# Scores of all heads in native fp32, two heads on the two row halves of the PE array

## The chip, the core and the metric

The program runs on one NeuronCore of a Trainium2 chip. The metric is the device time of one execution in microseconds (us). Five engines run their own instruction streams and wait for each other through semaphores: TensorE (PE; the weight loads of its matmuls are listed apart as PEld), VectorE (DVE), ScalarE (ACT), GpSimd (POOL) and SyncE (SP, which issues the DMAs here).

## What is computed

Causal attention for 4 batches of 12 heads, 448 positions and head size 64, then a gated feed-forward layer on the 1792 tokens. The inputs are float32 and the weights of the second part float64.

```python
scores = scale * np.matmul(q, k.transpose(0, 1, 3, 2))
mask = np.triu(np.ones((seq, seq), dtype=bool), k=1)
scores = np.where(mask, -1000000000.0, scores)
scores = scores - np.max(scores, axis=-1, keepdims=True)
attn = np.exp(scores)
attn = attn / (np.sum(attn, axis=-1, keepdims=True) + 1e-09)
out = np.matmul(attn, v)                  # (4, 12, 448, 64) -> x (1792, 768)
g = x @ w_gate                            # (768, 1536)
val = x @ w_val
y = (g * (1.0 / (1.0 + np.exp(-g))) * val) @ w_out
```

## The kernel before

**Chunks and units.** The work is cut into four chunks, one for each batch. A chunk has 12 attention units (one head each, taken two by two as pairs) and then a feed-forward part of 36 weight tiles (`moe`, L638). The feed-forward part of chunk c is meant to run together with the attention of chunk c+1, so that TensorE always has matmuls.

**A unit.** The 448 queries are cut into four blocks of 64, 128, 128 and 128 rows; block i needs the keys up to its own end (64, 192, 320, 448). For each block a score matmul fills an S bank of PSUM (L423), DVE adds the mask and takes the row maximum (L440), ACT takes the exponential with the row sums (L449), DVE adds and inverts the sums (L460, L461), and one of three engines scales the rows (L470, L474, L478). Then, for each block of keys j, TensorE transposes the probabilities into a T bank (L501), ACT copies them to SBUF (L268), in most units DVE writes the rest after rounding (L290), and the product with v is summed in an O bank (L514, or L533 and L535). The result is written into `xs`, the input of the feed-forward part.

**Two ways to keep float32 precision.** A matmul on float32 operands ("native") is slower for each column than one on `fp32r` operands (float32 rounded to fewer bits). So a product can also be split: an operand is written as a rounded part and a rest, and matmuls on the parts are summed. `NS` says pair by pair whether the scores are native ("n") or split ("s"): native in batch 0, split in batches 1 to 3. Both forms of a score matmul have 128 rows here. In the split form q is rounded into `QS` on rows 0 to 63 (L399), its rest goes to rows 64 to 127 (L400), k goes rounded into `KH` (L402) and its rest into `KL` (L403), and two matmuls with QS give the block (L429, L430). In the native form k is zero on rows 64 to 127, and one matmul gives the block (L426); the trace has two records for it. `NP` chooses in the same manner for the product with v. The feed-forward part is split throughout, three matmuls of 448 columns for a product (L634 to L636), which is why every weight tile is first rebuilt from float64 on DVE (L604, L608, L612; `wraw`) and split (`whl`: copy at L268 or L274, rest at L290 or L293) in chunk 0, stored to DRAM, and loaded again for the later chunks.

**The order.** The program for each engine is an order that a list scheduler written out in the kernel (`Planner`, L81) makes before the build. Each operation has one or more engines with an estimated cost (`cost`, L51), a due time, the operations that it needs, and the buffers that it takes; `CAPS` says how many buffers (or PSUM banks: S, T, O, M) a tag has. The scheduler gives each operation to the engine where it would end first, with a bias for each engine. Each engine then works through its list in that order.

**Loads.** q and k are given twice, on both halves of the partitions; a pair's q or k is one DMA of 128 rows x 2 heads x 448 (448 KB), but for the first pair, which is loaded head by head.

Of the kernel before, what the change touches and what calls it, by code (L numbers as in the profile page):

```python
# [15 lines left out]
D = 64  # L16
# [10 lines left out]
NS = ['nn', 's', 'sss', 'sss']  # L27
# [8 lines left out]
TM = 0  # L36
OM = 0
SM = 1
# [27 lines left out]
class Op:  # L66
    __slots__ = ("port", "soft", "alts", "due", "deps", "alloc", "uses", "extra", "idx", "nd", "outs", "start", "end", "eng", "fn")
# [13 lines left out]
class Planner:  # L81
# [9 lines left out]
    def run(self, caps):  # L91
        free = dict.fromkeys(("PE", "DVE", "ACT", "POOL", "SP"), 0.0)
        ring = {}
        lock = {"DVE": 0.0, "POOL": 0.0}

# [20 lines left out]
        def ready(o, e):  # L116
            t = 0.0
            for d in o.deps:
                x = d.end if d in o.soft else d.end + d.extra + (LAT if d.eng != e else (0.0 if e == "PE" else 0.1))
                if x > t:  # L120
                    t = x
            for r in o.alloc:
                q = slots(r.tag)
                h = q[0]
# [16 lines left out]
        def choose(e):  # L141
# [23 lines left out]
        while left:  # L165
# [10 lines left out]
            o.end = s + o.alts[e][0]  # L176
            o.fn = o.alts[e][1]
            free[e] = o.end
            if e == "POOL" or (e == "DVE" and o.port):
                lock[e] = o.end  # L180
# [4 lines left out]
            for r in o.uses:  # L185
                r.left -= 1
                r.end = max(r.end, o.end + o.extra + LAT)
# [14 lines left out]
def kernel(  # L202
# [9 lines left out]
    B, _, H, S = qT.shape  # L212
# [44 lines left out]
    def op(alts, due, deps=(), alloc=(), uses=(), extra=0.0):  # L257
# [3 lines left out]
        o.port = bool(alts.pop("port", False))  # L261
        for r in alloc:
            heads[r.tag] = o
# [33 lines left out]
    class Unit:  # L297
        def __init__(self, c, b, h, qa, qb, col):
# [6 lines left out]
            self.ns, self.np = nat(NS, b, h), nat(NP, b, h)  # L305
# [28 lines left out]
    loads = {}  # L334
    xs_ops, xs_res, xlast = {}, {}, {}

    def attention(u):
# [3 lines left out]
        ns, npv = U.ns, U.np  # L341
# [4 lines left out]
        if h % 2 == 0:  # L346
            def make(nm):
                if nm == "v":
                    t = buf([P, 2, NKC, D], F32, "vraw", "vraw", f"vraw{u}")[:, :, :nj]
                else:  # L350
                    t = buf([P, 2, S], F32, nm + "raw", nm + "raw", f"{nm}raw{u}")
                    t = t[:, :, :N] if nm == "q" else t[:, :, :KB]
                st[u][nm], st[u + 1][nm] = t[:, 0], t[:, 1]
                return t

            def src(nm, hs):
                if nm == "v":
                    return vP[b, :, hs, :nj]
                return qT[b, :, hs, U.qa : U.qb] if nm == "q" else kT[b, :, hs, :KB]

            def both(nm):
                def go():
                    t = make(nm)
                    nc.sync.dma_start(t, src(nm, slice(h, h + 2)))
                r = Res(nm + "raw")
                o = op({"SP": (0.6, go)}, base - 8.0, alloc=[r], extra=3.0)
                loads[u, nm] = loads[u + 1, nm] = (o, r)

            def one(nm, first):
                def go():  # L370
                    if first:
                        make(nm)
                    nc.sync.dma_start(st[u + 1 - first][nm], src(nm, h + 1 - first))
                if first:
                    r = Res(nm + "raw")
                    loads[u, nm] = (op({"SP": (0.6, go)}, base - 8.0, alloc=[r], extra=2.5), r)
                else:
                    o, r = loads[u, nm]
                    loads[u + 1, nm] = (op({"SP": (0.6, go)}, base - 8.0, [o], uses=[r], extra=2.5), r)

            if u == 0:
                for first in (1, 0):
                    for nm in "qk":
                        one(nm, first)
                both("v")
            else:
                for nm in "qkv":
                    both(nm)
# [4 lines left out]
        if not ns:  # L393
            rQ, rKH, rKL = Res("QS"), Res("KH"), Res("KL")

            def new(tag):
                s[tag] = buf([P, S], F32R, tag, tag, f"{tag}{u}")[:, : N if tag == "QS" else KB]
                return s[tag]
# [17 lines left out]
        exps, rps = [], {}  # L416
        for i, (q0, q1_) in U.qi:
            r, o0 = q1_ - q0, q0 - U.qa
            stag = "M" if c == 0 and SM and i == 3 else "S"
            sl = U.pslot(q1_)  # L420
            rS, rp = Res(stag), Res(f"p{sl}")

            def score(i=i, o0=o0, q1_=q1_, r=r, stag=stag):  # L423
                S_ = s[f"S{i}"] = bank(stag, f"S{u}_{i}")
                if ns:
                    nc.tensor.matmul(S_[:r, :q1_], s["q"][:, o0 : o0 + r], s["k"][:, :q1_], start=True, stop=True)  # L426
                else:
# [4 lines left out]
            if ns:  # L432
                so = op({"PE": (cost("PE", "n", q1_), score)}, due(2), [lq, lk], [rS], [rq, rk])
            else:
                so = op({"PE": (2 * cost("PE", "r", q1_), score)}, due(2), [q2, k2], [rS], [rQ, rKH, rKL])
# [48 lines left out]
        otag = "M" if c == 0 and OM and h % 2 else "O"  # L484
        rO = Res(otag)
        last = None
        pvs = []
        for j in range(nj):
            k0, k1_ = U.kb[j]
            bs, sl, stk = U.base(j), U.slot(j), U.stacked(j)  # L490
            kn, n = k1_ - k0, U.qb - bs
            lastj = j == nj - 1
            ttag = "M" if c == 0 and TM and j % 2 else "T"
            rT, rh = Res(ttag), Res(f"ph{sl}")
            qs = [(i, e) for i, e in U.qi if e[0] >= k0]

            def transp(j=j, k0=k0, k1_=k1_, kn=kn, ttag=ttag, qs=qs, bs=bs):
                pt = s[f"T{j}"] = bank(ttag, f"T{u}_{j}")
                for i, (q0, q1_) in qs:
                    r = q1_ - q0  # L500
                    nc.tensor.transpose(pt[:kn, q0 - bs : q1_ - bs], s[f"p{i}"][:r, k0:k1_], ident[:r, :r])  # L501
            tr = op({"PE": (sum(cost("PE", "t", max(kn, e[1] - e[0])) for _, e in qs), transp)}, due(7),
                    [norms[i] for i, _ in qs], [rT], [rps[i] for i, _ in qs])

            def newh(j=j, n=n, kn=kn, sl=sl):
                s[f"ph{j}"] = buf([P, S - WID[sl]], F32 if npv else F32R, f"ph{sl}", "ph", f"ph{u}_{j}")[:, :n]
                return s[f"ph{j}"][:kn]
            hi = op(copies("psum", n, newh, lambda j=j, kn=kn, n=n: s[f"T{j}"][:kn, :n],
                           engines="AD" if npv else "A"), due(8), [tr], [rh], [rT])
            if npv:  # L510
                def pv(j=j, kn=kn, bs=bs, lastj=lastj):
                    if j == 0:
                        s["O"] = bank(otag, f"O{u}")
                    nc.tensor.matmul(s["O"][:D, bs - U.qa : N], s["v"][:kn, j], s[f"ph{j}"][:kn],  # L514
                                     start=(j == 0), stop=lastj)
                pvs.append((cost("PE", "n", n), pv, [hi, lv], [rh, rv]))
                continue
            rl = None if stk else Res(f"pl{sl}")

            def newl(j=j, n=n, kn=kn, sl=sl, stk=stk):  # L520
                if stk:
                    return s[f"ph{j}"][kn : 2 * kn]
                s[f"pl{j}"] = buf([P, S - WID[sl]], F32R, f"pl{sl}", "pl", f"pl{u}_{j}")[:, :n]
                return s[f"pl{j}"][:kn]
            lo = op(binary(n, newl, lambda j=j, kn=kn, n=n: s[f"T{j}"][:kn, :n],
                           lambda j=j, kn=kn: raw(s[f"ph{j}"])[:kn], engines="D"),
                    due(9), [hi], [] if stk else [rl], [rT, rh])

            def pv(j=j, bs=bs, stk=stk, lastj=lastj):
# [249 lines left out]
```

## Time and profile before

| | us |
|---|---|
| median of 3 runs | 769.82 (769.75 to 773.38) |
| profiled execution | 767.99 |
| its span, first to last instruction | 766.2 |
| PE busy | 729.5 |
| DVE busy | 446.0 |
| ACT busy | 387.7 |
| POOL busy | 241.4 |

The profile is one execution. A busy time is the length of the union of an engine's records; records of matmuls overlap, so the time that a matmul costs is read from one start to the next start. In the rows below, "128\*64" behind a matmul is rows x columns of its stationary operand, and the last number of a shape is the columns that it streams. "x8" is a count of merged records; a row of merged records carries the shape of the first alone.

### The profile page before, as it was taken

The numbers are of one execution on the slowest core, as the hardware profiler recorded it, in microseconds if no ns is written. First come the engines' busy times: TensorE is split into PE (matmuls) and PEld (weight loads), VectorE is DVE, ScalarE is ACT, GpSimd is POOL, SyncE is SP. The second block draws the span as 40 slices with busy tenths as digits, with TensorE's granted clock in tenths as the row PEclk, the third lists the DMA queues.
The fourth block names the chain that finished last, engine by engine and source line by source line (L and its number), as shares of the span: only waits on it lengthen the run. The fifth ranks groups of instructions, "written<-read, shape, count | busy, mean of one in ns | idle before, by whom it ended". The sixth has DMA issues, their size and how long they took to land.

```text
span 766.2 us, 10921 instructions
## 1 busy us (share of the span) xinstructions
PE 729.5 (95%) x3798; PEld 632.2 (83%) x3798; DVE 446.0 (58%) x1009; ACT 387.7 (51%) x979; POOL 241.4 (32%) x291
## 2 busy tenths in 40 slices
PE   6999978788889899999999999999999999999998
PEld 3556867677768799998998999898998999999997
DVE  3878989998999875555564426556564322222100
ACT  5888566677767665445464435545455431111100
POOL 3577546455454463123232212322223100000000
PEclk9999999999999999999999999999999999999999
DMA  8645888687889986656556675655545566665672
GB/s 331 208 151 183 271 281 295 222 331 258 308 269 332 337 306 223 224 199 208 199 204 224 227 234 205 225 200 192 187 162 174 189 197 231 220 213 209 208 263 92
DMA packets 40087, 176.09 MB, mean 230 GB/s; under 512 B 4448, under 2 KB 8032, under 8 KB 40032
## 3 DMA queue, kind: packets, MB, share of 16 engines
q1 hardware_dynamic: 40032, 175.39, 66.3%
q8 instruction: 30, 0.49, 0.2%
q14 instruction: 25, 0.20, 0.1%
HBM read 141.56 MB, written 33.82 MB: 229 GB/s over the span
## 4 chain that ended last, share of the span: by engine, by line
PE 78%; DVE 11%; DMA 4%; ACT 3%; issue 2%; POOL 1%; SPq 0%; POOLq 0%; ACTq 0%; DVEq 0%
PE M L634 13%; PE M L636 12%; PE M L635 12%; PE T L501 7%; PE MO L634 7%; PE MO L636 7%; PE MO L635 7%; DVE wraw L608 3%; PE S L426 3%; PE O L533 3%; DVE wraw L612 2%; PE S L429 2%; PE S L430 2%; PE O L535 2%; DMA wide<-in_w_dram 2%
## 5 line engine op out<-in xcount | busy, mean ns | idle before, releaser
L636 PE MATMUL M<-xh,whl 128*128 128x448 f32 x576 | 212.0, 368 | 7.5 <-DVE whl L290 7.5
L634 PE MATMUL M<-xh,whl 128*128 128x448 f32 x576 | 215.8, 375 | 0.0
L635 PE MATMUL M<-xl,whl 128*128 128x448 f32 x576 | 211.1, 366 | 0.5 <-DVE xl L290 0.5
L636 PEld LDWEIGHTS M<-xh,whl 128*128 128x128 f32 x576 | 108.5, 188 | 19.4 <-DVE whl L290 10.4
L449 ACT ACTIVATE p<-p,m 64x64 f32<-64x64 f32 x192 | 95.9, 501 | 40.7 <-DVE m L440 40.5
L635 PEld LDWEIGHTS M<-xl,whl 128*128 128x128 f32 x576 | 108.9, 189 | 8.6 <-DVE xl L290 0.9
L634 PEld LDWEIGHTS M<-xh,whl 128*128 128x128 f32 x576 | 109.0, 189 | 7.6 <-issue 0.2
L268 ACT ACTIVATE ph<-T 64x448 fp32r<-64x448 f32 (+1 forms) x192 | 72.6, 416 | 79.6 <-PE T L501 78.3
L440 DVE CUSTOM_DVE_ANT_0 p<-S,mask 64x64 f32<-64x64 f32 x192 | 76.5, 417 | 61.3 <-PE S L430 42.7
L636 PE MATMUL MO<-hh,whl 128*128 128x448 f32 x288 | 106.0, 368 | 4.3 <-DVE whl L290 4.2
L634 PE MATMUL MO<-hh,whl 128*128 128x448 f32 x288 | 107.5, 373 | 0.0
L635 PE MATMUL MO<-hl,whl 128*128 128x448 f32 x288 | 105.5, 366 | 0.0
L501 PE MATMUL T<-ident,p 128*128 128x128 f32 (+2 forms) x480 | 80.2, 279 | 10.3 <-DVE ph L290 5.4
L501 PEld LDWEIGHTS T<-ident,p 128*128 128x128 f32 (+2 forms) x480 | 53.2, 130 | 44.5 <-issue 12.0
L474 POOL TENSOR_SCALAR p<-p,rec 128x448 f32<-128x448 f32 (+3 forms) x77 | 45.0, 594 | 74.3 <-DVE rec L461 56.9
L290 DVE TENSOR_TENSOR pl<-T,ph 128x384 fp32r<-128x384 f32 (+2 forms) x126 | 50.1, 419 | 23.8 <-ACT ph L268 22.6
L636 PEld LDWEIGHTS MO<-hh,whl 128*128 128x128 f32 x288 | 54.2, 188 | 10.2 <-DVE whl L290 5.3
L670 DVE SCALAR_TENSOR_TENSOR t<-t,M 128x448 f32<-128x448 f32 x48 | 29.6, 618 | 49.1 <-ACT t L666 48.8
L635 PEld LDWEIGHTS MO<-hl,whl 128*128 128x128 f32 x288 | 54.4, 189 | 4.0
L634 PEld LDWEIGHTS MO<-hh,whl 128*128 128x128 f32 x288 | 54.4, 189 | 3.8
L268 ACT ACTIVATE hh<-t 128x448 fp32r<-128x448 f32 x42 | 24.2, 576 | 63.0 <-DVE t L676 63.0
L470 ACT ACTIVATE p<-p,rec 128x320 f32<-128x320 f32 (+3 forms) x115 | 48.8, 475 | 12.3 <-DVE rec L461 12.3
(61 smaller groups left out, 1051.3 us busy)
## 6 DMA issues: line engine op xcount, KB each, us to landing
whl<-ws SPq DMA_DIRECT2D x108, 768.0 KB, 4.3
wide<-in_w_dram SPq DMA_DIRECT2D x36, 768.0 KB, 6.4
ws<-whl SPq DMA_DIRECT2D x36, 768.0 KB, 7.1
qraw<-in_q_dram SPq DMA_DIRECT2D x23, 448.0 KB, 4.2
kraw<-in_k_dram SPq DMA_DIRECT2D x23, 448.0 KB, 4.7
vraw<-in_v_dram SPq DMA_DIRECT2D x24, 256.0 KB, 4.5
out_dram<-osb SPq DMA_DIRECT2D x24, 224.0 KB, 4.8
qraw<-in_q_dram SPq DMA_DIRECT2D x2, 224.0 KB, 4.5
```

Of the source, the lines that this page charges most:

```text
L268: nc.scalar.activation(out(), in_(), AF.Copy, scale=scale)
L290: r["DVE"] = (cost("DVE", "two", n), lambda: nc.vector.tensor_tensor(out(), a(), b(), alu))
L426: nc.tensor.matmul(S_[:r, :q1_], s["q"][:, o0 : o0 + r], s["k"][:, :q1_], start=True, stop=True)
L440: nc.vector.tensor_tensor_reduce(p[:r], s[f"S{i}"][:r, :q1_], mask[:r, maskX - q0 : maskX - q0 + q1_], -0.125, 3.0e38, ALU.add, ALU.min, m ...
L449: nc.scalar.activation(p[:r], p[:r], AF.Exp, bias=s[f"m{i}"][:r], scale=-1.0, accum_out=sums[u % NR][:r, i : i + 1],)
L470: nc.scalar.activation(p[:r], p[:r], AF.Copy, scale=rec[u % NR][:r, i : i + 1])
L474: nc.gpsimd.tensor_scalar(p[:r], p[:r], rec[u % NR][:r, i : i + 1], 0.0, ALU.mult, ALU.add)
L501: nc.tensor.transpose(pt[:kn, q0 - bs : q1_ - bs], s[f"p{i}"][:r, k0:k1_], ident[:r, :r])
L634: nc.tensor.matmul(out[:, :n], a[:, w], xhi, start=first, stop=False)
L635: nc.tensor.matmul(out[:, :n], a[:, w], xlo, start=False, stop=False)
L636: nc.tensor.matmul(out[:, :n], l[:, w], xhi, start=False, stop=last)
L670: nc.vector.scalar_tensor_tensor(t, t, 1.0, ps[c, f, 0][:, :N], ALU.add, ALU.mult)
```

## The change

All scores become native. q and k are laid out so that head 2g stands on partitions 0 to 63 and head 2g+1 on partitions 64 to 127; nothing is duplicated or padded with zeros. The scores of a block are one operation for both heads: two matmuls with 64 rows each, one behind the other, the first on the upper and the second on the lower row half, each into its own S bank. The operation takes both of its banks at once. `QS`, `KH`, `KL`, their four split operations and `NS` are gone, and a pair's q or k is one DMA of 224 KB. In chunk 0 the odd blocks take their two banks from the M banks.

Along with it go other edits. The transposes of key blocks 2 and 3 share one T bank, with one copy and one rest operation for both (`groups`). T has 3 banks instead of 2, O has 1 instead of 2. qraw has 3 buffers, whl 6. The scheduler gets a delay for each engine (`LAT`), a price for a change between transposes and other matmuls (`TURN`) with a preference for a further transpose, and a model of the transfers' time (`KBUS`, `DLAT`).

```diff
-NS = ['nn', 's', 'sss', 'sss']
-LAT = 0.2
+LAT = {"PE": 0.29, "DVE": 0.2, "ACT": 0.23, "POOL": 0.2, "SP": 0.1}
+TURN = 0.088
-WLAT = 5.0
-CAPS = {'S': 2, 'T': 2, 'O': 2, 'M': 2, 'qraw': 2, 'kraw': 3, 'vraw': 3, 'QS': 1, 'KH': 2, 'KL': 2, 'VS': 2, 'ph': 2, 'pl': 2, 'p': 3, 'tmp': 2, 't': 3, 'osb': 2, 'wide': 3, 'wraw': 3, 'whl': 4}
+KBUS = 1 / 320
+DLAT = 1.8
+CAPS = {'S': 2, 'T': 3, 'O': 1, 'M': 2, 'qraw': 3, 'kraw': 3, 'vraw': 3, 'VS': 2, 'ph': 2, 'pl': 2, 'p': 3, 'tmp': 2, 't': 3, 'osb': 2, 'wide': 3, 'wraw': 3, 'whl': 6}
...
+            if e == "PE" and kind == "t":
+                for s, o in cand:
+                    if s <= lim and o.kind == "t":
+                        return s, o
...
-            q1 = op(copies("sbuf", N, lambda: new("QS"), lambda: s["q"]), due(0), [lq], [rQ], [rq])
-            q2 = op(binary(N, lambda: s["QS"][D:P], lambda: s["q"][D:P], lambda: raw(s["QS"])[D:P]),
-                    due(1), [q1], [], [rQ, rq])
-            k1 = op(copies("sbuf", KB, lambda: new("KH"), lambda: s["k"]), due(0), [lk], [rKH], [rk])
-            k2 = op(binary(KB, lambda: new("KL"), lambda: s["k"], lambda: raw(s["KH"])),
-                    due(1), [k1], [rKL], [rKH, rk])
...
+        if h % 2 == 0:
+            for i, (q0, q1_) in U.qi:
+                stag = "M" if c == 0 and i % 2 else "S"
+                rSs = [Res(stag), Res(stag)]
+                def score(i=i, q0=q0, q1_=q1_, stag=stag):
+                    for v in (u, u + 1):
+                        st[v][f"S{i}"] = bank(stag, f"S{v}_{i}")
+                    for v in (u, u + 1):
+                        nc.tensor.matmul(st[v][f"S{i}"][: q1_ - q0, :q1_], st[v]["q"][:, q0:q1_], st[v]["k"][:, :q1_],
+                                         start=True, stop=True)
+                so = op({"PE": (cost("PE", "n", q1_) + 0.1, score)}, due(2), [lq, lk], rSs, [rq, rk])
...
-                if ns:
-                    nc.tensor.matmul(S_[:r, :q1_], s["q"][:, o0 : o0 + r], s["k"][:, :q1_], start=True, stop=True)
-                else:
-                    QS = s["QS"][:, o0 : o0 + r]
-                    nc.tensor.matmul(S_[:r, :q1_], QS, s["KH"][:, :q1_], start=True, stop=False)
-                    nc.tensor.matmul(S_[:r, :q1_], QS, s["KL"][:, :q1_], start=False, stop=True)
...
+        groups = [[0], [1], [2, 3]]
+        for g, js in enumerate(groups):
...
+            hi = op(copies("psum", n, newh, lambda g=g, kn=kn, n=n: s[f"T{g}"][:kn, :n],
                            engines="AD" if npv else "A"), due(8), [tr], [rh], [rT])
...
-    def dup_t(a):
-        t = a.transpose(0, 3, 1, 2)
-        return _np.concatenate([t, t], axis=1)
+    def pairs(a):
+        return a.reshape(B, H // 2, 2, S, Dh).transpose(0, 2, 4, 1, 3).reshape(B, 2 * Dh, H // 2, S)
```

## Rows read from the trace of the kernel before

**Rows 1.** The page's first part: span, then busy us (share) and instructions by engine.
```profile
span 766.2 us, 10921 instructions
...
PE 729.5 (95%) x3798; PEld 632.2 (83%) x3798; DVE 446.0 (58%) x1009; ACT 387.7 (51%) x979; POOL 241.4 (32%) x291
```

**Rows 2.** Windows: length, busy us (count) of PE, PEld, DVE, ACT, POOL; clock; DMA.
```profile
0.00:80.00 80.00, 72.24 (x337) 45.24 (x338) 57.89 (x186) 63.84 (x194) 48.24 (x73) 1.00 0.62 218
80.00:285.00 205.00, 179.64 (x919) 152.68 (x918) 187.78 (x315) 135.82 (x301) 107.67 (x85) 0.98 0.84 295
285.00:457.50 172.50, 172.47 (x950) 156.24 (x949) 89.71 (x238) 85.51 (x229) 46.22 (x73) 1.00 0.64 216
457.50:630.20 172.70, 172.70 (x950) 156.37 (x949) 88.23 (x235) 85.25 (x227) 39.27 (x62) 1.00 0.57 192
630.20:766.20 136.00, 132.49 (x650) 121.64 (x648) 22.42 (x36) 17.31 (x31) 0.00 (x0) 1.00 0.59 204
```

**Rows 3.** Windows again, of the middle of the first stage alone.
```profile
17.00:62.60 45.60, 45.08 (x227) 27.99 (x226) 38.22 (x126) 41.01 (x129) 30.64 (x46) 1.00 0.51 173
```

**Rows 4.** Waits of 80 to 285 us: who for whom, us, times, longest.
```profile
PEld M L636 <- DVE whl L290: 10.4, 8, 2.2
...
PE M L636 <- DVE whl L290: 7.5, 7, 1.9
```

**Rows 5.** Timeline of PE, first 22 us: start, us, instruction, count, idle before.
```profile
4.00 3.95 PE L426 MATMUL S<-kraw,qraw 128*64 128x64 f32 x8 [4.00 <-DMA kraw<-in_k_dram]
10.62 6.66 PE L426 MATMUL S<-kraw,qraw 128*64 128x64 f32 x16 [2.66 <-DMA kraw<-in_k_dram]
```

**Rows 6.** Timeline of PE: one unit's native scores, then a transpose.
```profile
24.66 2.09 PE L426 MATMUL S<-kraw,qraw 128*64 128x64 f32 x8
26.68 1.02 PE L501 MATMUL T<-ident,p 64*64 64x64 f32 x7
```

**Rows 7.** Timeline of PE: one unit's split scores between feed-forward matmuls.
```profile
314.44 0.19 PE L429 MATMUL S<-KH,QS 128*64 128x64 f32 x1
...
314.80 0.39 PE L634 MATMUL M<-xh,whl 128*128 128x448 f32 x1
...
315.43 0.31 PE L429 MATMUL S<-KH,QS 128*128 128x320 f32 x1
...
316.13 0.37 PE L634 MATMUL M<-xh,whl 128*128 128x448 f32 x1
```

**Rows 8.** Timeline of PE: a run of transposes between feed-forward matmuls.
```profile
307.06 0.37 PE L636 MATMUL M<-xh,whl 128*128 128x448 f32 x1
307.36 1.02 PE L501 MATMUL T<-ident,p 64*64 64x64 f32 x7
308.13 0.45 PE L634 MATMUL M<-xh,whl 128*128 128x448 f32 x1
...
308.42 0.36 PE L635 MATMUL M<-xl,whl 128*128 128x448 f32 x1
```

**Rows 9.** Windows of the instructions on QS, then of those on KH.
```profile
80.00:285.00 205.00, 17.06 (x88) 12.89 (x88) 0.62 (x1) 3.45 (x6) 18.79 (x16) 0.98 0.84 295
...
80.00:285.00 205.00, 12.81 (x44) 7.98 (x44) 0.00 (x0) 5.65 (x10) 18.98 (x13) 0.98 0.84 295
```

**Rows 10.** Groups of DVE by shape: count, busy us, mean ns, idle before.
```profile
L290 DVE TENSOR_TENSOR pl<-T,ph 128x384 fp32r<-128x384 f32 x42 | 23.4, 557 | 1.1
...
L290 DVE TENSOR_TENSOR pl<-T,ph 128x256 fp32r<-128x256 f32 x42 | 17.7, 420 | 20.3 <-ACT ph L268 20.2
...
L290 DVE TENSOR_TENSOR pl<-T,ph 128x128 fp32r<-128x128 f32 x42 | 11.8, 282 | 2.4 <-ACT ph L268 2.4
```

**Rows 11.** Groups, 80 to 285 us: the rests of weight tiles, DVE, POOL.
```profile
L290 DVE TENSOR_TENSOR whl<-wraw,whl 128x768 fp32r<-128x768 f32 x22 | 23.4, 1065 | 0.0
...
L293 POOL TENSOR_TENSOR whl<-wraw,whl 128x768 fp32r<-128x768 f32 x11 | 21.6, 1963 | 33.4 <-ACT whl L268 28.1 <-DMA wide<-in_w_dram 5.3
```

**Rows 12.** One line's instructions: count, ns min/median/max, first and last start.
```profile
L608 DVE SCALAR_TENSOR_TENSOR wraw<-wide,wraw x36: 927/960/2984, 21.6 to 267.5; 128x768 uint32<-128x768 uint32 x36
```

More of the change, by code (lines that the diff above doesn't have):

```diff
@@ L66 @@
 class Op:
[L67 removed]
+    __slots__ = ("port", "kind", "soft", "kb", "alts", "due", "deps", "alloc", "uses", "extra", "idx", "nd", "outs", "start", "end", "eng", "fn")
     def __init__(self, alts, due, deps, alloc, uses, extra):
@@ L118, in ready @@
             for d in o.deps:
-                x = d.end if d in o.soft else d.end + d.extra + (LAT if d.eng != e else (0.0 if e == "PE" else 0.1))
+                x = d.end if d in o.soft else d.end + d.extra + (LAT[d.eng] if d.eng != e else (0.0 if e == "PE" else 0.13))
                 if x > t:
                     t = x
-            for r in o.alloc:
-                q = slots(r.tag)
-                h = q[0]
+            for i, r in enumerate(o.alloc):
+                h = slots(r.tag)[sum(x.tag == r.tag for x in o.alloc[:i])]
                 if h is not None:
@@ L333 @@
     st = [dict() for _ in range(NU)]
-    loads = {}
+    loads, scored = {}, {}
     xs_ops, xs_res, xlast = {}, {}, {}
@@ L363, in go @@
                     t = make(nm)
-                    nc.sync.dma_start(t, src(nm, slice(h, h + 2)))
+                    src = vP[b, :, h : h + 2, :nj] if nm == "v" else (qT if nm == "q" else kT)[b, :, h // 2]
+                    nc.sync.dma_start(t, src)
                 r = Res(nm + "raw")
-                o = op({"SP": (0.6, go)}, base - 8.0, alloc=[r], extra=3.0)
+                o = op({"SP": (0.3, go), "kb": 256 if nm == "v" else 224}, base - 8.0, alloc=[r])
                 loads[u, nm] = loads[u + 1, nm] = (o, r)
[L369 to L376, printed above, removed]
-                else:
[L378 to L388, printed above, removed]
+            for nm in "qkv":
+                both(nm)
         lq, rq = loads[u, "q"]
@@ L482, in attention @@
             }, due(6), [rc], [], [rps[i], rsum])
-        otag = "M" if c == 0 and OM and h % 2 else "O"
-        rO = Res(otag)
+        rO = Res("O")
         last = None
         pvs = []
[L488 to L508, printed above, removed]
@@ L518, in attention @@
[L518 to L527, printed above, removed]
@@ L529, in pv @@
-            def pv(j=j, bs=bs, stk=stk, lastj=lastj):
-                if j == 0:
-                    s["O"] = bank(otag, f"O{u}")
-                O, V = s["O"][:, bs - U.qa : N], s["VS"][:, j, :]
-                nc.tensor.matmul(O, V, s[f"ph{j}"], start=(j == 0), stop=stk and lastj)
-                if not stk:
-                    nc.tensor.matmul(O, V, s[f"pl{j}"], start=False, stop=lastj)
-            pvs.append(((1 if stk else 2) * cost("PE", "r", n), pv, [hi, lo, v2], [rh, rV] + ([] if stk else [rl])))
+                for j, o_, w in zip(js, offs, cols):
+                    def pv(g=g, j=j, o_=o_, w=w, kn=kn):
+                        if j == 0:
+                            s["O"] = bank("O", f"O{u}")
+                        nc.tensor.matmul(s["O"][:D, U.base(j) - U.qa : N], s["v"][:kn, j],
+                                         s[f"ph{g}"][:kn, o_ : o_ + w], start=(j == 0), stop=(j == nj - 1))
+                    pvs.append((cost("PE", "n", w), pv, [hi, lv], [rh, rv]))
@@ new lines, in attention, with pv @@
+            for j, o_, w in zip(js, offs, cols):
+                def pv(g=g, j=j, o_=o_, w=w, stk=stk):
+                    if j == 0:
+                        s["O"] = bank("O", f"O{u}")
+                    O, V = s["O"][:, U.base(j) - U.qa : N], s["VS"][:, j, :]
+                    lastj = j == nj - 1
+                    nc.tensor.matmul(O, V, s[f"ph{g}"][:, o_ : o_ + w], start=(j == 0), stop=stk and lastj)
+                    if not stk:
+                        nc.tensor.matmul(O, V, s[f"pl{g}"][:, o_ : o_ + w], start=False, stop=lastj)
+                pvs.append(((1 if stk else 2) * cost("PE", "r", w), pv, [hi, lo, v2], [rh, rV] + ([] if stk else [rl])))
@@ L768 @@
     nc = _bacc.Bacc("TRN2", target_bir_lowering=False, num_devices=1)
-    for name, a in (("q", dup_t(q)), ("k", kt), ("v", vp), ("w", wp)):
+    for name, a in (("q", pairs(q)), ("k", pairs(k)), ("v", vp), ("w", wp)):
         a = _np.ascontiguousarray(a)
```

100 lines of the change are left out of this document (56 added, 44 removed).

## The prediction

> **What bounds the kernel now.** I read the page's first part for the shares, then windows cut where the feed-forward parts begin and end, then the waits inside the one stage where PE has gaps, then the timeline of PE for what a score block costs from start to start. The profiled execution took 768.0 us, 1.8 above its span [rows 1]; the median of the runs is 1.8 above it. I make the sum against 768.0 and add 1.8 at the end.
>
> The windows give five stages [rows 2]. A, 0 to 80: attention of batch 0, hardly any feed-forward work. B, 80 to 285: the first feed-forward part, the rebuilding of the weights, attention of batch 1. C and D, to 457.5 and 630.2: feed-forward part and attention of the next batch. E: the last feed-forward part alone. The share of 95% for PE hides that they have different limits:
> - In C and D PE is busy 172.5 of 172.5 and 172.7 of 172.7 us, DVE and ACT about half. There only PE work counts, each us of it.
> - In E PE has 650 records in 132.5 us, 0.204 each: feed-forward matmuls, which the change doesn't touch.
> - In B DVE is busy 187.8 of 205 us and PE 179.6. PE's missing 25.4 us are waits, the longest of them for DVE's rests of weight tiles [rows 4]. DVE sets the pace.
> - In A, between 17 and 62.6 us, PE is busy 45.1 of 45.6 us, ACT 41.0 and DVE 38.2 [rows 3]. PE is first, ACT close behind.
>
> **What a score block costs, old and new.** A unit's native scores start at 24.66 and the next transpose at 26.68 [rows 6]: 2.02 us, in which one exit to transposes lies. Such a change shows in rows 8: the feed-forward matmul ahead of the transposes takes 0.30 instead of 0.20 to the next start, the first one behind them 0.29. So about 0.09 of the 2.02 is the change, and a native unit is 1.93. A split unit is 0.36 + 0.70 = 1.06 us [rows 7], a pair of them 2.12.
>
> No row shows two matmuls on two row halves, so the new pair is bounded from both sides. If the halves run at the same time, a pair costs one native unit, 1.93 (I see nothing that would make it less, since a head still streams all its columns). If they run one after the other it is 3.86. The nearest row is that of matmuls already in flight together: a feed-forward record is 0.36 long [rows 8] while the next starts 0.20 later [rows 2], so PE does hold several at once, and here the two have no row, no operand and no bank in common. I take 1.93. The Trainium skill, "TensorEngine Tiling (Array Packing)", Key Properties, says that tiles work independently and can do weight loads and matmuls in parallel; by that it would be 1.93 as well.
>
> Then the entries into and exits out of the 64-row form. The nearest row is the entry into a run that begins with a 64x64 transpose, 0.10 [rows 8]; the exit is bounded by 0 and the same 0.10 (the split blocks show no gap between 64 and 128 columns [rows 7], but that is no change of rows). I take 0.15 for each block that stands alone between other matmuls, 0.6 for a pair's four. The same page says that changing the tiling mode drains the engine; the 0.10 is this case's size of it.
>
> **Stage by stage.**
> - A, scores. Six pairs go from 2 x 2.02 = 4.04 to 1.93 + 0.4 (two entries and exits at most, since nothing need stand between the blocks) = 2.33: 6 x 1.71 = 10.3 us less on PE. Beside it, the start: the first head's blocks begin at 4.00, then PE waits 2.66 us for the second head's k, and three heads are scored only by 17.28 [rows 5]. Now both heads come in one transfer of the size that one head had, and the next pair's q and k are 448 KB instead of 896: the 2.66 go. Together 13 us on PE. But ACT was busy 41.0 of 45.6 us [rows 3] and keeps its exponentials; over the whole stage it has 16.2 us free [rows 2]. I take 10, between 5 and 14.
> - B, DVE. Split work on DVE itself: 0.6 us [rows 9]. Merging blocks 2 and 3 turns 0.420 + 0.282 into 0.557 [rows 10]: 0.145 x 12 units = 1.7. So 2.3 for certain. The larger part is indirect: POOL loses 18.8 + 19.0 = 37.8 us and ACT 9.1 [rows 9]. The rests of weight tiles may run on DVE (22, 23.4 us) or POOL (1.96 us each) [rows 11]; should eleven go over, DVE loses another 11 x 1.065 = 11.7 and POOL gains 21.6, which fits. DVE's rebuilding steps also stretch from 0.93 to up to 2.98 us [rows 12], which I put down to POOL's two-input work beside them; as other such work takes the freed place I count nothing. B gains 2.3 to 17 (PE's 25.4 us of gaps are more than that); I take 9. PE's scores here change by what C shows, inside the gaps.
> - C and D. A pair goes from 2.12 to 1.93 + 0.6 = 2.53: 6 x 0.41 = 2.5 us more. One run of transposes fewer in a unit saves up to 0.09 x 12 = 1.1. So +1.4 in each stage, +3 together, between -2 (blocks side by side, entries shared) and +5. The split operations that go lie on engines that are half idle there: nothing.
> - E: nothing.
> - Small edits: qraw, whl and the halved loads are hidden in C and D, where PE never waits; their cover in B is the wait for DVE. The scheduler's new constants reorder everything; C and D, two orders of the same work, differ by 0.2 us, so I count 0, plus or minus 3.
> - The new wait: an operation takes two S banks at once, so the next block stands behind two row maxima on DVE instead of one. Behind it in PE's list stand feed-forward matmuls. In C a unit has 172.5 / 12 = 14.4 us, so nothing waits. In A banks S and M take turns.
>
> Sum: -10 - 9 + 3 = -16, 768.0 - 16 = 752, and with the 1.8 to the median 753.8.
>
> **Rivals.**
> 1. Starts in order (23%). A head's block is two records, one after the other on the same rows; if the second head's first can't start before the first head's second has, a pair takes 1.5 x 1.93 = 2.9. Against it: nothing in the two heads depends on each other. For it: every stretch of PE that I read has starts in program order, and a head's two records stand together in the list. Then C and D pay 6 x (2.9 + 0.6 - 2.12) - 1.1 = 7.2 each, A gains 6 x (4.04 - 3.3) + 2.7 less ACT = 6, and B gains 5, as PE's own part grows by 8 inside the gaps: 768.0 + 14.4 - 11 = 771.4, median 773. Without the B gain 778. This is slower, and it decides once a pair, its entries with it, costs more than about 3.2 us in C and D, since 12 x (3.2 - 2.12) - 2.2 = 10.8 is what A and B give there. The rule stands in the Trainium skill, "TensorE: Matmul & The Clock Gate", What overlaps and what doesn't: matmuls start and end strictly in program order, and only weight loads are pulled ahead. No run here shows it for two halves.
> 2. No overlap (10%): the halves run one after the other and the change doesn't do what it says. C and D pay 6 x (3.86 + 0.6 - 2.12) - 1.1 = 13 each, A gains 2, B 0: 792, median 794.
> 3. Overlap, but A's gain is eaten (10%): with one O bank the products with v of a unit wait until the unit before has been copied out, 0.6 us of DVE and the way there and back, 12 times; up to 10 us. Then only B and +3 stand: 762, median 764, inside or near no change.
>
> **How the numbers follow.** Forecast 57%, its own range 738 to 767. The predicted time is its 753.8. The range that should hold 8 in 10 leaves out the second rival (10%) and the lower tail of the forecast (both A and B at their best ends, 14 + 17 us): 738 to 781. A difference of 0.5%, 3.8 us, is about what a measurement of this kernel can tell from none. Faster by more: 54 of the forecast's 57, 4 of rival 3, 2 of rival 1: 60%. Within: 3 of the forecast, 5 of rival 3, 10 of rival 1, which lies on the edge: 18%. Slower: 11 of rival 1, 1 of rival 3, all of rival 2: 22%.
>
> **What would show it.** On PE, the two heads' score records of one block should lie side by side, and a pair's four blocks together hold PE for 1.9 to 2.5 us; in rival 1 the second head's first record starts with the first head's second and the four blocks take about 3.5; in rival 2 the four records stand in a row, 4.5. Stage A should end near 70 us, B last some 196, C and D 172 to 175 each, E 136. In B the rests of the weights should move from DVE to POOL, and DVE's busy time there fall by some 10 us. The prediction is wrong if C or D is over 178 us (PE price of a pair), if A still ends after 77 (ACT or the O bank), or if B keeps its 205 (DVE not relieved).

## The result, and the profile after

The changed kernel takes 746.85 us (median of four runs, 746.45 to 748.23), the kernel before 769.79 in the same comparison: a ratio of 0.9702, 95% interval 0.9661 to 0.9743. The prediction was 753.8, with a range of 738 to 781.

The page's first part shows the same work on PE in a shorter span, and less on the three other engines.

```profile
span 744.3 us, 10630 instructions
...
PE 728.5 (98%) x3798; PEld 608.1 (82%) x3798; DVE 389.8 (52%) x933; ACT 353.5 (47%) x891; POOL 181.1 (24%) x221
```

PE's busy time fell by 1.0 us only, its idle time by 20.9 us (36.7 to 15.8, the span less the busy time of [rows 1] and of this page). The windows of the changed kernel, cut at the same events (columns as in [rows 2]):

```profile
0.00:72.20 72.20, 65.46 (x352) 41.28 (x352) 57.31 (x192) 63.23 (x187) 44.06 (x66) 1.00 0.66 227
72.20:250.90 178.70, 173.26 (x907) 145.94 (x907) 162.60 (x299) 118.63 (x264) 80.08 (x62) 0.99 0.84 305
250.90:429.30 178.40, 178.40 (x945) 149.52 (x945) 72.82 (x201) 75.52 (x202) 31.61 (x51) 1.00 0.60 203
429.30:608.30 179.00, 179.00 (x950) 149.75 (x950) 74.61 (x207) 78.84 (x208) 25.35 (x43) 1.00 0.53 178
608.30:744.30 136.00, 132.35 (x649) 121.58 (x647) 22.44 (x36) 17.30 (x31) 0.00 (x0) 1.00 0.57 192
```

Stage A ends here where the last part of `xl` of batch 0 is written, the others where the last matmul of a feed-forward part starts; by these marks A of the kernel before lasted 81.7 us and B 203.4:

```profile
0.00:81.70 81.70, 73.48 (x342) 46.04 (x342) 59.59 (x187) 65.53 (x197) 49.45 (x73) 1.00 0.63 220
81.70:285.10 203.40, 178.50 (x913) 151.97 (x913) 186.08 (x314) 134.23 (x296) 106.55 (x84) 0.97 0.83 295
```

So A lost 9.5 us, B 24.7, C gained 5.8 and D 6.4, E nothing: -22.0, the span's -21.9. Two things stand out. B lost far more than predicted, and it now lasts as long as C: with 5.4 us of gaps left on PE, B has come down to PE's own work. And C and D, where PE was busy all the time before, grew more than predicted: both passed the 178 us that the prediction had set as a sign that its price of a pair on PE is wrong.

That the two halves run together is seen at the very start. The first row is PE's list up to 4.10 us, the second the whole first stretch:

```profile
3.99 0.37 PE L403 MATMUL S<-kraw,qraw 64*64 64x64 f32 x2 [3.99 <-DMA kraw<-in_k_dram]
```
```profile
3.99 4.41 PE L403 MATMUL S<-kraw,qraw 64*64 64x64 f32 x20 [3.99 <-DMA kraw<-in_k_dram]
```

Two records of 0.34 and 0.36 us start within 0.01 us of each other; the next two, the ones that signal that a head's matmul is done, start only at 4.12 and 4.15. So the first two are the first records of the two heads. Four blocks of both heads and the first block of the next pair (20 records) are done by 8.40; before, one head's four blocks took until 7.95 and the second head's started at 10.62 [rows 5].

### The profile page after: what moved, and what is told of

Same layout as the page of the kernel before. It is cut to its first block, busy times and chain, and to the rows that moved or that the text cites. A ratio compares the mean times of both kernels' runs of the same rounds, so it can differ in the third digit from the quotient of the medians.

```text
span 744.3 us, 10630 instructions
## 1 busy us (share of the span) xinstructions
PE 728.5 (98%) x3798; PEld 608.1 (82%) x3798; DVE 389.8 (52%) x933; ACT 353.5 (47%) x891; POOL 181.1 (24%) x221
## 4 chain that ended last, share of the span: by engine, by line
PE 86%; DVE 6%; ACT 2%; DMA 2%; issue 1%; POOL 1%; SPq 0%; ACTq 0%
PE M L615 15%; PE M L617 14%; PE M L616 14%; PE MO L615 9%; PE MO L617 8%; PE MO L616 8%; PE T L477 7%; PE S L403 6%; PE O L514 3%; PE O L516 2%; PE O L494 2%; DMA wide<-in_w_dram 2%; DVE wraw L589 2%; DVE wraw L593 1%; DVE p L416 1%
## 5 line engine op out<-in xcount | busy, mean ns | idle before, releaser
L615 PEld LDWEIGHTS M<-xh,whl 128*128 128x128 f32 x576 | 108.8, 189 | 24.7 <-issue 14.4
L425 ACT ACTIVATE p<-p,m 64x64 f32<-64x64 f32 (+3 forms) x192 | 96.0, 502 | 69.3 <-DVE m L416 68.9
L416 DVE CUSTOM_DVE_ANT_0 p<-S,mask 64x64 f32<-64x64 f32 (+1 forms) x192 | 74.5, 417 | 77.7 <-PE S L403 75.5
L279 ACT ACTIVATE ph<-T 128x384 fp32r<-128x384 f32 (+2 forms) x143 | 61.4, 495 | 40.2 <-PE T L477 39.7
L450 POOL TENSOR_SCALAR p<-p,rec 128x320 f32<-128x320 f32 (+3 forms) x68 | 41.6, 624 | 141.2 <-DVE rec L437 127.4
L403 PE MATMUL S<-kraw,qraw 64*64 64x64 f32 (+3 forms) x384 | 69.2, 440 | 6.3 <-DMA kraw<-in_k_dram 4.0
L477 PE MATMUL T<-ident,p 128*128 128x128 f32 (+2 forms) x480 | 67.0, 276 | 1.4 <-POOL p L450 0.8
L477 PEld LDWEIGHTS T<-ident,p 128*128 128x128 f32 (+2 forms) x480 | 50.8, 130 | 19.6 <-issue 9.8
L279 ACT ACTIVATE hh<-t 128x448 fp32r<-128x448 f32 x39 | 22.5, 577 | 77.4 <-DVE t L657 77.4
L657 DVE TENSOR_TENSOR t<-t,M 128x448 f32<-128x448 f32 x48 | 29.7, 620 | 50.8 <-PE M L617 50.4
```

The costliest lines, as they stand in the source:

```text
L279: nc.scalar.activation(out(), in_(), AF.Copy, scale=scale)
L403: nc.tensor.matmul(st[v][f"S{i}"][: q1_ - q0, :q1_], st[v]["q"][:, q0:q1_], st[v]["k"][:, :q1_], start=True, stop=True)
L416: nc.vector.tensor_tensor_reduce(p[:r], s[f"S{i}"][:r, :q1_], mask[:r, maskX - q0 : maskX - q0 + q1_], -0.125, 3.0e38, ALU.add, ALU.min, m ...
L425: nc.scalar.activation(p[:r], p[:r], AF.Exp, bias=s[f"m{i}"][:r], scale=-1.0, accum_out=sums[u % NR][:r, i : i + 1],)
L450: nc.gpsimd.tensor_scalar(p[:r], p[:r], rec[u % NR][:r, i : i + 1], 0.0, ALU.mult, ALU.add)
L477: nc.tensor.transpose(pt[:kn, o_ + q0 - bs : o_ + q1_ - bs], s[f"p{i}"][:r, U.kb[j][0] : U.kb[j][1]], ident[:r, :r])
```

## The experiments

Times are medians, with ratios to the kernel before in the same comparison. Stages are cut at the same events throughout, in the profiled execution of each run. x4 is one run only. Of `CAPS` the code cuts below print the changed entries alone.

| | us | A + B | A | B | C | D | DVE busy in B |
|---|---|---|---|---|---|---|---|
| before | 769.8 | 285.1 | 81.7 | 203.4 | 172.6 | 172.6 | 186.1 |
| changed | 746.9 | 250.9 | 72.2 | 178.7 | 178.4 | 179.0 | 162.6 |
| x2: pairs alone | 763.7 | 266.9 | 72.9 | 194.0 | 178.8 | 178.8 | 178.4 |
| x1: the other edits alone | 763.8 | 282.0 | 87.8 | 194.2 | 172.2 | 172.7 | 179.7 |
| x9: changed, old delays and transfer times | 759.6 | 263.2 | 75.9 | 187.3 | 178.9 | 178.9 | 167.2 |
| x11: changed, old transfer times | 756.0 | 259.3 | 72.4 | 186.9 | 178.9 | 179.1 | 166.9 |
| x5: changed, whl 4 | 747.4 | 250.8 | 71.4 | 179.4 | 178.9 | 179.0 | 163.9 |
| x8: changed, no merged transposes | 746.3 | 252.7 | 72.1 | 180.6 | 178.9 | 179.0 | 166.3 |
| x4: changed, both heads on the same rows | 788.3 | 271.9 | 89.2 | 182.7 | 189.2 | 189.2 | 163.4 |
| x6: changed, two blocks in a bank | 733.9 | 244.7 | 72.0 | 172.7 | 175.6 | 175.5 | 160.9 |
| x7: x6, first block 128 wide | 733.3 | 245.1 | 71.9 | 173.2 | 175.2 | 175.2 | 162.5 |
| x3: changed, split again in batches 2 and 3 | 738.2 | 256.2 | 71.5 | 184.7 | 171.9 | 172.8 | 168.6 |
| x10: x7, split again in batches 2 and 3 | 731.1 | 247.7 | 70.5 | 177.2 | 172.5 | 172.8 | 169.2 |

**Which part brought what: x1 and x2.** Theory 1: the pairs bring the gain. Rival: the edits beside them do. In `MODE` a letter stands for each batch: N is native with 128 rows, S is split, P is pairs.

```diff
 x1, from the changed kernel: the scores in their old form again
+MODE = 'NSSS'
-'whl': 6
+'whl': 4, 'QS': 1, 'KH': 2, 'KL': 2
...
 x2, from the kernel before: the scores alone
+                for v in (u, u + 1):
+                    nc.tensor.matmul(st[v][f"S{i}"][: q1_ - q0, :q1_], st[v]["q"][:, q0:q1_], st[v]["k"][:, :q1_],
+                                     start=True, stop=True)
```

> The changed kernel with only the scores put back to their old form: native with 128 rows in batch 0, split in batches 1 to 3 (QS, KH, KL and their four operations back, q and k loaded twice). The other edits stay (delays, transfer model, merged transposes, 3 T banks, 1 O bank), but whl has 4 buffers, since 6 no longer fit. Stages of the changed kernel: A to 72.2, B 178.7, C 178.4, D 179.0, E 136.1 us. Theory 1 (the pairs brought the gain of A and B, by taking work off PE in A and off POOL, ACT and DVE in B): A 78 to 80, B 195 to 205, C and D 171 to 173, in all 756 to 768. Theory 2 (the other edits brought it): A 72 to 76, B 178 to 185, C and D 171 to 173, in all 730 to 742, faster than the changed kernel.

> The kernel before with only the scores changed: pairs on the two row halves, q and k unsplit, in all batches; scheduler constants, banks, buffers and transposes as before. Theory 1 (the pairs bring the gain): A 70 to 74, B 176 to 190, C and D 178 to 181 each, in all 740 to 756. Theory 2 (the other edits bring it): A 74 to 80, B 198 to 206, C and D 179 to 181, in all 766 to 780.

Measured: 763.8 (ratio 0.9931, 0.9911 to 0.9950) and 763.7 (0.9927, 0.9900 to 0.9954). Neither theory stands alone: each part gives 6 us, both together 23. The windows of x2, A to D:

```profile
0.00:72.90 72.90, 64.10 (x339) 37.88 (x340) 55.58 (x185) 61.12 (x188) 41.26 (x63) 0.98 0.54 191
72.90:266.90 194.00, 181.70 (x917) 146.06 (x916) 178.43 (x312) 126.52 (x284) 85.24 (x70) 0.99 0.83 293
266.90:445.70 178.80, 178.80 (x950) 149.22 (x949) 75.70 (x218) 77.20 (x215) 31.32 (x53) 1.00 0.57 194
445.70:624.50 178.80, 178.80 (x950) 149.11 (x949) 77.06 (x220) 80.50 (x218) 25.11 (x44) 1.00 0.52 179
```

The pairs alone take 8.8 us from A and 9.4 from B, and give 6.2 back in C and again in D. The other edits alone take 3.1 from A and B together (A gets longer, B shorter) and leave C and D as they were. Put on top of the pairs, the same edits take 16.0 from A and B.

In B of x2 the rests of the weight tiles do move to POOL, as foretold, but five of them and not eleven: 16 on POOL and 17 on DVE, where [rows 11] have 11 and 22.

```profile
L289 DVE TENSOR_TENSOR whl<-wraw,whl 128x768 fp32r<-128x768 f32 x17 | 17.1, 1006 | 0.5 <-POOL whl L273 0.5
```
```profile
L292 POOL TENSOR_TENSOR whl<-wraw,whl 128x768 fp32r<-128x768 f32 x16 | 30.4, 1900 | 35.9 <-ACT whl L267 35.8
```

In the changed kernel itself they hardly move: 19 on DVE and 12 on POOL. What falls there is DVE's rebuilding of the weights, of which the prediction had said that it counts nothing. Its two longer steps, in B of x2 and then of the changed kernel:

```profile
L578 DVE SCALAR_TENSOR_TENSOR wraw<-wide,wraw 128x768 uint32<-128x768 uint32 x31 | 41.8, 1350 | 0.7
L582 DVE SCALAR_TENSOR_TENSOR wraw<-wide,wraw 128x768 uint32<-128x768 uint32 x31 | 37.9, 1221 | 0.6
```
```profile
L589 DVE SCALAR_TENSOR_TENSOR wraw<-wide,wraw 128x768 uint32<-128x768 uint32 x30 | 35.4, 1181 | 0.0
L593 DVE SCALAR_TENSOR_TENSOR wraw<-wide,wraw 128x768 uint32<-128x768 uint32 x30 | 31.8, 1061 | 0.1
L301 DVE TENSOR_TENSOR whl<-wraw,whl 128x768 fp32r<-128x768 f32 x19 | 18.1, 950 | 0.8 <-ACT whl L279 0.8
...
L304 POOL TENSOR_TENSOR whl<-wraw,whl 128x768 fp32r<-128x768 f32 x12 | 25.4, 2120 | 28.5 <-ACT whl L279 23.4 <-DVE wraw L585 4.9
```

These two steps, one of each fewer, take 12.5 us less in the changed kernel, of the 15.8 us by which DVE's busy time in B falls from x2 to it. The pairs alone left them as they were (81.1 in the kernel before, 79.7 in x2). In x1, x8, x9 and x11 they are short too (means of 1.05 to 1.16), so they don't need the pairs, the merged transposes or the new delays and transfer times to be short; which edit shortens them isn't shown.

**Which of the other edits: x5, x8, x9, x11.** Three candidates: deeper weight buffers, merged transposes, the scheduler's delays and transfer times. The fixed time `fix` is 3.0 us for q, k and v, 4.5 for `wide`, 5.0 for `ws` and `whl`, 2.5 for the output; x9 also takes the old delay of 0.1 us (0.13 in the change) within an engine.

```diff
 x5
-'whl': 6
+'whl': 4
 x8
-        groups = [[0], [1], [2, 3]]
+        groups = [[0], [1], [2], [3]]
 x9 and x11 (in x11 LAT stays as changed)
-LAT = {"PE": 0.29, "DVE": 0.2, "ACT": 0.23, "POOL": 0.2, "SP": 0.1}
+LAT = {"PE": 0.2, "DVE": 0.2, "ACT": 0.2, "POOL": 0.2, "SP": 0.2}
-                wire = max(wire, o.end) + o.kb * KBUS
-                o.extra = wire + DLAT - o.end
+                o.end += 0.3
+                free[e] = o.end
+                o.extra = o.fix
```

> The changed kernel with 4 buffers for whl instead of 6, nothing else. The two parts of the change apart gave 6 us each, together 23, so 11 us come only from both. Theory 1 (the room that QS, KH and KL leave goes to whl, and the deeper weight buffers free B's rebuilding): A and B together 256 to 262 instead of 250.9, C and D unchanged, in all 752 to 758. Theory 2 (the buffers are not it): within 2 us of 746.9.

> The changed kernel with the transposes of key blocks 2 and 3 in two T banks again, with two copies and two rests. Theory 1 (the merge takes one ACT and one DVE operation from each unit, 0.17 and 0.145 us, which counts in A and B, and at most one change to transposes on PE): A and B 2 to 6 us longer, C and D up to 1 each, in all 749 to 755. Theory 2 (the merge is the larger part of what only both parts gave): 756 or more.

> The changed kernel with the scheduler's old delays and its old fixed times for transfers (one delay of 0.2 us between all engines, 0.6 us to issue a DMA and 2.5 to 5 us until it has landed), TURN and the rest as in the change. Theory 1 (the better order, with the true delays, is what lets A and B use the engines that the pairs free): A and B 256 to 264, C and D 178 to 180, in all 752 to 760. Theory 2 (the delays matter little): within 3 us of 746.9.

> The changed kernel with the old fixed transfer times alone; the new delays between engines stay. Old delays and old transfer times together gave 759.6 us, 12.7 longer. Theory 1 (the transfers' model is it: the old one thinks loads later than they are, and so orders the rebuilding of the weights later): 755 to 760. Theory 2 (the delays between engines are it): 745 to 750.

Measured: 747.4 (0.9727, 0.9686 to 0.9769), 746.3 (0.9717, 0.9681 to 0.9754), 759.6 (0.9885, 0.9850 to 0.9921) and 756.0 (0.9834, 0.9800 to 0.9869). The buffers and the merged transposes are worth nothing that can be measured: for the merge my expectation of 749 to 755 was wrong. The old delays and times cost 12.7 us, 9.1 of them by the transfer times alone, those nearly all in B. The expectation of x11 named the wrong direction: a weight tile (`wide`) takes 5.4 us from issue to landing in the median of x11 and up to 9.0, where the old scheduler counts on a fixed 5.1 (0.6 for the issue and 4.5 behind it). So it thinks loads earlier than they are, by little in the median and by more for the slow ones; the new formula gives 4.5 (0.3 + 768 / 320 + 1.8) for a load alone and more behind other transfers. The landing of `wide` in x11:

```profile
DMA to landing us min/median/max: 4.1/5.4/9.0
```

Engines then reach work whose tile isn't there. The waits of the tile's first readers in B, of the kernel before, of x11 and of the changed kernel (us in total, times, longest):

```profile
ACT wide L268 <- DMA wide<-in_w_dram: 17.7, 14, 3.8
POOL wide L274 <- DMA wide<-in_w_dram: 10.3, 4, 3.2
```
```profile
ACT wide L281 <- DMA wide<-in_w_dram: 15.4, 12, 3.7
POOL wide L287 <- DMA wide<-in_w_dram: 9.0, 4, 4.4
```
```profile
POOL wide L285 <- DMA wide<-in_w_dram: 6.5, 2, 4.0
ACT wide L279 <- DMA wide<-in_w_dram: 4.7, 4, 1.6
```

28.0, 24.4 and 11.2 us. That these waits fall is shown; that they are the cause of the 9.1 us is not, and x2 speaks against it. It has the old times too, waits 16.0 us for the tile in B, and its B is 7.1 us longer than that of x11:

```profile
ACT wide L267 <- DMA wide<-in_w_dram: 10.7, 9, 2.1
POOL wide L273 <- DMA wide<-in_w_dram: 5.3, 3, 3.1
```

**Do the halves run together: x4.**

```diff
-                    t = buf([P, S], F32, nm + "raw", nm + "raw", f"{nm}raw{u}")
-                    st[u][nm], st[u + 1][nm] = t[:D], t[D:]
+                    t = buf([P, 2, S], F32, nm + "raw", nm + "raw", f"{nm}raw{u}")
+                    st[u][nm], st[u + 1][nm] = t[:D, 0], t[:D, 1]
```

> The changed kernel with both heads of a pair on partitions 0 to 63 (each score matmul still has 64 rows, so the entries and exits stay), so that the two heads can't run at the same time; qraw has 2 buffers, as the tiles are twice as wide. Theory 1 (the halves run together, which saves a pair's columns once, 1.71 us): C and D 10 us longer each, 187 to 190, A 8 to 12 longer, in all 775 to 785. Theory 2 (the halves only look as if they ran together, each at half its speed): C and D within 2 us of 179, in all 745 to 752.

A single run: 788.3 us, C and D 189.2 as theory 1 has it. A is 17.0 us longer, where 8 to 12 were expected, and so the whole is 3 us above the expected 785. The block of 448 columns in C, of the changed kernel and of x4, each with the matmul ahead of it and two behind it:

```profile
315.64 0.36 PE L617 MATMUL M<-xh,whl 128*128 128x448 f32 x1
315.93 1.02 PE L403 MATMUL S<-kraw,qraw 64*128 64x448 f32 x4
316.88 0.47 PE L615 MATMUL M<-xh,whl 128*128 128x448 f32 x1
317.19 0.36 PE L616 MATMUL M<-xl,whl 128*128 128x448 f32 x1
```
```profile
311.22 0.36 PE L617 MATMUL M<-xh,whl 128*128 128x448 f32 x1
311.51 1.77 PE L403 MATMUL S<-kraw,qraw 64*128 64x448 f32 x4
313.21 0.47 PE L615 MATMUL M<-xh,whl 128*128 128x448 f32 x1
313.51 0.36 PE L616 MATMUL M<-xl,whl 128*128 128x448 f32 x1
```

From the block's start to the next matmul it is 0.95 us on two halves and 1.70 on the same rows: the second head costs 0.75, all its columns, in x4, and nothing in the changed kernel. So theory 1 stands, and both rivals on overlap fall; a single run is enough here, as the rows themselves and 10 us in each of two stages say the same. The same rows give the price of a visit. The columns are 0.75 of the 0.95, which leaves 0.20; the matmul ahead takes 0.29 to the next start and the first one behind 0.31, against 0.20 between neighbours. 0.20 + 0.09 + 0.11 = 0.40 us for each block that stands alone, where I had counted 0.15.

**Is it the visit that costs: x6 and x7.** A bank holds 512 columns, so blocks of 64 and 448 columns fit in one, and 192 and 320 in another. x6 scores two blocks in one operation, back to back.

```diff
 x6
+            for g, ids in enumerate(((0, 3), (1, 2))):
+                stag = "M" if c == 0 and g else "S"
+                rSs = [Res(stag), Res(stag)]
...
+                    for i, (q0, q1_) in blks:
+                        for v in (u, u + 1):
+                            nc.tensor.matmul(st[v][f"S{i}"][: q1_ - q0, :q1_], st[v]["q"][:, q0:q1_],
+                                             st[v]["k"][:, :q1_], start=True, stop=True)
 x7: the first block with 128 columns of q
-nc.tensor.matmul(st[v][f"S{i}"][: q1_ - q0, :q1_], st[v]["q"][:, q0:q1_],
+nc.tensor.matmul(st[v][f"S{i}"][:, :q1_], st[v]["q"][:, q0 : q0 + P],
```

> The changed kernel with a pair's four score blocks in two operations instead of four: blocks of 64 and 448 columns share one bank for each head, and blocks of 192 and 320, so two blocks stand back to back on PE. In the changed kernel a block that stands alone between feed-forward matmuls costs 0.39 us more than its columns: 0.09 to enter, 0.20 before the next start, 0.10 on the one after. Theory 1 (this is the price of the entry into and exit from the 64-row form, once for each visit): two visits a pair fewer, 0.78 us, 6 pairs: C and D 4.7 us shorter, 173.5 to 174.5 each, in all 734 to 739. Theory 2 (each block pays it, by its own weight loads or by the two heads hindering each other): C and D stay at 178 to 179, in all 744 to 748.

> The kernel with two score blocks in one bank (733.9 us), with the 64-row first block's matmul given 128 columns of q instead of 64 (the 64 further rows of the result are not read), so that the visit of the blocks of 64 and 448 columns no longer changes from 64x64 to 64x128 in its middle. There the second block now starts 0.10 us after the first has streamed, and its first record is 0.10 longer. Theory 1 (a change of the tile's columns costs as much as a change of its rows): 0.2 us a pair less, C and D 1 to 1.5 us shorter than 175.6 and 175.5, in all 730 to 733. Theory 2 (the two pay for something else, such as the weights' load of 128 columns): no change, 733 to 735.

x6 takes 733.9 us (0.9551, 0.9524 to 0.9578), C and D 175.6 and 175.5: 2.8 and 3.5 us less than in the changed kernel, against 4.7 expected. Its two visits in C:

```profile
274.66 1.28 PE L408 MATMUL S<-kraw,qraw 64*64 64x64 f32 x8
275.87 0.47 PE L621 MATMUL M<-xh,whl 128*128 128x448 f32 x1
...
278.52 1.13 PE L408 MATMUL S<-kraw,qraw 64*128 64x192 f32 x8
279.58 0.47 PE L621 MATMUL M<-xh,whl 128*128 128x448 f32 x1
```

The second visit, 192 and 320 columns, holds PE for 1.06 us from start to start; in the changed kernel the two blocks took 0.53 and 0.74, so 0.21 is saved there, and 0.20 of entry and exit beside it. The first, 64 and 448, takes 1.21, no less than 0.26 and 0.95 apart. So the second visit pays 0.40 once, as theory 1 has it; in the first only the 0.20 on the neighbours is saved, and 0.20 stays. Six pairs with 0.60 each make 3.6 us, close to the 2.8 and 3.5. Of the 13.0 us of x6 6.0 are in B; why B falls by more than its six pairs' 3.6 isn't shown.

Is the 0.20 that stays the step from a 64x64 to a 64x128 tile in the middle of the first visit? x7 takes that step away: the visit became 1.18 instead of 1.21, and the kernel takes 733.3 (0.9531, 0.9505 to 0.9557), which is no difference to x6. That is theory 2 of x7: the step is not shown to cost anything. The weight loads, of 128 columns for a block of 64 in x7, may be it (such a load takes 0.19 us in these traces), but that is argued, not shown.

**Pairs only where PE is not alone the bound: x3 and x10.**

```diff
 x3, from the changed kernel
+MODE = 'PPSS'
-'whl': 6
+'whl': 4, 'QS': 1, 'KH': 2, 'KL': 2
 x10, from x7
+MODE = 'PPSS'
-'qraw': 3, 'kraw': 3, 'whl': 6
+'qraw': 2, 'kraw': 2, 'whl': 5, 'QS': 1, 'KH': 2, 'KL': 2
```

> The changed kernel with pairs in batches 0 and 1 and split scores in batches 2 and 3 (whl 4 buffers, since 6 no longer fit). Theory 1 (pairs help where PE is not alone the bound, and cost 1.15 us a pair where it is): A and B as in the changed kernel, 72 and 177 to 182, C and D back to 171 to 173, in all 731 to 738. Theory 2 (the split scores cost as much in C and D by other ways now, or the four whl buffers slow B): 742 to 752.

> The same with pairs in batches 0 and 1 alone and split scores in batches 2 and 3 (whl 5, qraw 2, kraw 2 buffers, so that it fits). Theory 1 (pairs where other engines matter, split scores where PE alone counts): A and B 245 to 252, C and D 172 to 173, in all 727 to 734. Theory 2 (the split operations of batch 2's first pairs fall into B and cost there what C and D give): 735 to 740.

x3 takes 738.2 us (0.9603, 0.9574 to 0.9632): C and D come back to 171.9 and 172.8, and B pays 6.0 of it. Having 4 buffers for whl costs B 0.7 us in x5. The rest may come from the split operations of batch 2's first pairs, which fall into B, or from the order that changes with them; no run parts these. x10 takes 731.1 us (0.9508, 0.9483 to 0.9533), the lowest median here, though only 2.2 us below x7, whose interval overlaps with its own. Again C and D fall, by 2.7 and 2.4 against x7, and B pays 4.0.

## Why the prediction was right, and where it wasn't

**The bound of each stage: right.** C and D moved with PE's work alone (x4: +10.8 and +10.2 us, for 6 x 1.7 us of columns), E not at all, and A with PE. B went with DVE: from the kernel before to x2 DVE's busy time in B falls by 7.7 us and B by 9.4, to the changed kernel by 23.5 and 24.7. In x9 and x11 the two part somewhat (18.9 and 16.1, 19.2 and 16.5).

**Overlap: right.** A pair costs one native unit in columns, as assumed without a row for it. The rival with starts in order and the one without overlap are both out, by the first record rows and by x4. The Trainium skill, "TensorE: Matmul & The Clock Gate", What overlaps and what doesn't, has matmuls start strictly in program order. The program gives one head's matmul and then the other's, and a head's second record starts after the other head's first; as far as a head's two records are neighbours in the list that runs, which the trace can't tell, the measurement speaks against the rule between row halves.

**A: right, -9.5 against -10.** x2 gives -8.8 with the pairs alone. The sum had 13 us on PE and took 10 because of ACT; the wait of 2.66 us for the second head's k is gone, but that ACT kept the other 3.5 us isn't shown. The single O bank, the third rival, isn't seen: x2, with two O banks, has an A of 72.9 against 72.2, and PE's waits in A for the copy out of the O bank add up to 1.5 us in the changed kernel.

**B: right for the pairs, wrong in the sum.** The pairs give 9.4 in x2 where I had 9, though with five moved rests and not eleven, so the size was partly luck. The step that failed is the small edits, counted as 0, plus or minus 3, because C and D "differ by 0.2 us". That argument holds for stages where PE alone counts, and C and D did stay within 0.5 us. It says nothing of B, whose engines wait for each other. There, on top of the pairs, the edits give 15.3 us (x2 to the changed kernel), and 0.7 in A. Putting the old delays and transfer times back costs 12.7 us (x9), the transfer times alone 9.1 (x11). One row was there to warn: 17.7 and 10.3 us of waits for `wide` stood among B's waits, and I looked at PE's own waits only [rows 4]. They don't give the size, as x2 shows. x9 is still 3.7 us shorter in A and B than x2 (A 3.0 longer, B 6.7 shorter); where that comes from is open, and the banks, the third qraw buffer and the price for changes to transposes were not tried apart. The moved rests, the term by which the larger part of the 9 was reached, are not what relieved the changed kernel: one went over to POOL, and DVE's rebuilding steps, put at nothing, became shorter.

Why these edits give 3.1 us without the pairs and 16.0 with them is settled in part. Of the 12.9 us between, 6.8 are in A, which the edits without the pairs make 6.1 us longer. x1 stalls near its start: its second head is scored from 19.01 on, where the kernel before has it at 10.62 [rows 5], and from 16.6 to 26.9 us PE is busy half the time, at a mean granted clock of 0.67. PE's waits in x1, then that window of x1 and of the kernel before:

```profile
19.01 1.96 PE L453 MATMUL S<-kraw,qraw 128*64 128x64 f32 x6 [2.11 <-DMA kraw<-in_k_dram]
24.03 7.29 PE L453 MATMUL S<-kraw,qraw 128*128 128x320 f32 x20 [3.06 <-DVE m L468]
```
```profile
16.60:26.90 10.30, 5.13 (x13) 2.02 (x12) 7.01 (x15) 5.37 (x12) 2.71 (x3) 0.67 0.58 200
```
```profile
16.60:26.90 10.30, 10.30 (x49) 5.54 (x48) 8.53 (x29) 8.69 (x28) 6.01 (x8) 1.00 0.64 230
```

That is 5.2 us of PE's time. The other 6.1 us are in B and stay open. In x1, B has DVE busy 179.7 of 194.2 us and in the changed kernel 162.6 of 178.7, so DVE is as full in both; a better order can't give what the split work takes. That fits, but no run shows it. The granted clock differs as well: its mean in B is 0.97 in the kernel before and 0.96 in x1, 0.98 in x11, and 0.99 in x2, x9 and the changed kernel. By these means it can account for at most some 4 us of B's 24.7 (0.02 x 203, an estimate from the windows) and 2 of the 9.1 of x11; the prediction had no term for it.

**C and D: the sign was right, the size not.** +1.4 each was predicted, with +5 for both as the worst; measured are +5.8 and +6.4. The term is the entry and exit of a block, 0.15 us in the sum and 0.40 in the trace. I had taken the entry from [rows 8], 0.10 where it is 0.09, and put the exit at 0.05, half of a bound of 0.10; it is 0.31, 0.20 before the next start and 0.11 in the first matmul behind it, and the second of these stood in [rows 8] already. 6 x 4 x 0.25 = 6.0 us. On the other side the columns of a pair are 1.71 by the 0.75 for 448 and not 1.93, 1.3 us for six pairs. With the 2.5 of the sum this makes 7.2, 1 us more than the 5.8 to 6.4; that rest isn't explained. The four blocks of a pair hold PE for 2.48 us (0.26, 0.53, 0.74 and 0.95 to the next start), inside the 1.9 to 2.5 foretold; the matmuls ahead and behind add 0.8 to it, so a pair costs 3.28 where the sum had 2.53. The saving of 1.1 by merged transposes didn't come (x8: 0 to 0.5). The Trainium skill, "TensorEngine Tiling (Array Packing)", Key Properties, says that a change of mode drains the engine; this case fits that, with 0.40 us for a block that stands alone.

**In sum**, two terms were mis-sized in opposite ways: B by 15.7 us too little, C and D by 9.2 too little on the other side (12.2 where 3 were predicted). They cancel for the greater part, so -16 missed the -22.0 of the stages by 6, less than either term was off: that the forecast came so near was in good part luck.

## What to carry to other kernels

Put matmuls with 64 rows side by side on the two row halves when the columns count, but give each visit to that form as many blocks as a bank holds: here a visit cost 0.40 us, and two blocks in a bank gave 13 us, about half of them in the stages that PE alone bounds. Where PE is the only bound, a form that costs other engines more and PE less may still be the better one. When a change also touches a scheduler's estimates, test them in the stage whose engines wait for each other, and don't take their size from a stage where one engine hides every order.

## What the runs showed of the hardware

- Two 64-row float32 matmuls on different row halves start within 0.01 us of each other and take no longer than one: 0.95 us a block against 1.70 on the same rows.
- Going from 128-row to 64-row tiles and back costs 0.40 us for a block that stands alone: 0.09 before, 0.20 at the end, 0.11 in the next matmul. A second block of 64x128 tiles behind one of 64x128 tiles adds its columns alone (1.06 us for two blocks that take 0.53 and 0.74 apart); behind one of 64x64 tiles it saved none of its 0.20 (1.21 for 0.26 and 0.95).
